# When a fused attention and feed-forward kernel makes the hidden layer of its next step: always a step ahead, or only while weights are converted

## The chip, the core and the metric

The kernel runs on one core of a Trainium2 chip. The core has a matmul engine (PE, with its weight loads shown as PEld), a vector engine (DVE), a scalar engine (ACT), GpSimd (POOL) and a queue for transfers (SP). The metric is the device time of one execution in microseconds; the time before is the median of three runs.

## What is computed

The reference is a chain of three parts: attention with a decay instead of a softmax, a feed-forward layer with the activation h * tanh(softplus(h)), and a layer of 8 experts with a greedy assignment of tokens that respects a capacity. All is float32. The change touches the second part, for which the first part delivers x.

```python
scores = scale * np.matmul(q, k.transpose(0, 1, 3, 2))
ret = scores * Dmat[None, :, :, :]          # decay, causal
x = np.matmul(ret, v)                       # -> 2304 tokens x 512
...
h = x @ w_in                                # 512 -> 2048
sp = np.where(h > 20.0, h, np.log1p(np.exp(np.minimum(h, 20.0))))
g = h * np.tanh(sp)
y = g @ w_out                               # 2048 -> 512
...
out[mask] = np.maximum(y[mask] @ w1[e], 0.0) @ w2[e]    # per expert e
```

## The kernel before

The kernel has a first part (attention and feed-forward, `first_part`) and a second one (ranking of tokens and experts). The first part takes tokens in 9 blocks n of 256 and the 2048 hidden features in 16 groups f of 128. One pair (n, f) is a step; `plan` (line 65) puts the 144 steps in order: the first 48 mix the blocks 0 to 2, while the weights of the layer still arrive and are converted, and from step 48 on the blocks follow one another. All matmuls work on float32 split into a high and a low part, three products for one.

A step is a chain through all engines:

- `ff_h` (line 310): PE makes h, 12 matmuls into half a PSUM bank `ph`. The halves of one bank hold an even step and the odd one behind it; there are two such banks, `ph0` and `ph1`. An h of an odd step waits for the tanh of the even one in its bank; an h of an even step waits until the products of the two steps that used the bank last are made (`ff_b2`, line 353).
- `ff_a1` (line 322): ACT takes tanh, a square and a scaling (lines 327 to 329) into `d`, DVE multiplies the halves of `d` (line 335). `ff_a2`: DVE takes the reciprocal (line 340).
- `ff_b1` (line 342): POOL makes two products (lines 347, 348). `ff_b2`: DVE makes the activation's value (line 353).
- `ff_b3` (line 355): ACT rounds it to `gh` (line 359), POOL makes the rest `gl` (line 360).
- `ff_y` (line 398): PE multiplies both with the second weight and accumulates y, 6 matmuls of 512 columns (line 412), or 12 of 256 in the last block (line 448). The matmuls with `gh` come first, those with `gl` fifth and sixth; in the last block `gl` is in every third.

The loop (line 532) is the order written out by hand; each engine executes its instructions in the order in which they are issued. In turn i it issues, in this sequence: the slots of step i (pieces of attention for later blocks, of router logits and the like, with matmuls on PE and evictions on ACT and DVE), `ff_a1` of step i, `ff_h` of step i + 1, `ff_b3` of step i - 2, `ff_a2` of step i, `ff_b2` of step i - 1, `ff_b1` of step i, and `ff_y` of step i - 3. So h is made one turn ahead of its elementwise work. The first h is made in turn 0.

While weights are converted, which takes much of ACT and DVE, `now` or `old` holds a conversion. By `CONV` (line 58) and the 32 pieces, the last conversion is taken up in turn 28; `now` or `old` is set in turns 0 to 30. In these turns POOL's share of the elementwise work lies on DVE.

Of the kernel before, what the change touches and what calls it, by code (L numbers as in the profile page):

```python
# [64 lines left out]
def plan():  # L65


    spread = lambda a, b, n: [a + (b - a) * k // (n - 1) for k in range(n)]
    own = {i: (0, f) for f, i in enumerate([0, 1, 2, 3] + spread(6, ENDS[0], NF - 4))}
    free = [i for i in range(3 * NF) if i not in own]  # L70
    lead = [i for i in free if i < BEGIN2]
    rest = [i for i in free if BEGIN2 <= i]
    near = [i for i in rest if i <= ENDS[1]]
    ones = lead + [near[k] for k in spread(1, len(near) - 1, NF - len(lead))]
    own.update({i: (1, f) for f, i in enumerate(ones)})
    own.update({i: (2, f) for f, i in enumerate(i for i in free if i not in ones)})
    steps = [own[i] for i in range(3 * NF)]
    steps += [(n, f) for n in range(3, NB) for f in range(NF)]
    return steps


def first_part(ctx, tc, att, att_ht, att_hn, dtab, qtab, ktab, stab, wi, wo, wgb, ydram, L, constants, cst, begin, grid):
# [16 lines left out]
    steps = plan()  # L99
# [42 lines left out]
    class convert:  # L142
# [18 lines left out]
        def x(self):  # L161
            w0 = self.w0
            nc.vector.scalar_tensor_tensor(w0, self.w1, 0x80000000, w0, op0=ALU.bitwise_and,  # L163
                                           op1=ALU.bitwise_or)
# [16 lines left out]
    def x_block(n):  # L181
        if n not in xT:
            if n == 2:
                xT[n] = [sp.tile([P, KT, TB], F32R, tag="x2", name=f"x{k}2", bufs=2) for k in "hl"]
            else:
                xT[n] = [work.tile([P, KT, TB], F32R, tag="x" + k, name="x" + k, bufs=2) for k in "hl"]
        return xT[n]
# [117 lines left out]
    q2 = {}  # L305
# [4 lines left out]
    def ff_h(n, f, i):  # L310
        xh, xl = x_block(n)
        if i % 2 == 0:
            hbank[0] = psum.tile([P, 2, TB], F32, tag=("ph0", "ph1")[i // 2 % 2], name="ph")
        ph = hbank[0][:, i % 2, :]
        k = 0
        for kt in range(KT):
            for w, x in ((winh, xh), (winl, xh), (winh, xl)):
                nc.tensor.matmul(ph, w[f][:, kt, :], x[:, kt, :], start=(k == 0), stop=(k == 11))  # L318
                k += 1
        q2[n, f] = ph  # L320

    def ff_a1(n, f, i, alone):

        ph = q2[n, f]
        d = work.tile([P, 2, P], F32, tag="d", name="d", bufs=2)
        df = d.rearrange("p a b -> p (a b)")
        nc.scalar.activation(df, ph, AF.Tanh, scale=0.5)  # L327
        nc.scalar.activation(df, df, AF.Square, bias=half_b, scale=-0.5)  # L328
        nc.scalar.activation(df, df, AF.Copy, bias=0.5, scale=0.5)  # L329
        u = work.tile([P, 2, P], F32, tag="u", name="u", bufs=3)  # L330
        r = u[:, 0, :]
        if alone:

            r = rs[:, i % 2 * P:][:, :P]
        nc.vector.tensor_mul(r, d[:, 0, :], d[:, 1, :])  # L335
        inv[n, f] = (d, u, r, alone)

    def ff_a2(n, f):
        r = inv[n, f][2]
        nc.vector.reciprocal(r, r)  # L340

    def ff_b1(n, f, eng):
        d, u, r, alone = inv.pop((n, f))
        if alone:
            eng.tensor_mul(u, d[:, ::-1, :], r[:, None, :].to_broadcast([P, 2, P]))
        else:
            eng.tensor_mul(u[:, 1, :], d[:, 0, :], r)  # L347
            eng.tensor_mul(u[:, 0, :], d[:, 1, :], r)  # L348
        gt[n, f] = u.rearrange("p a b -> p (a b)")

    def ff_b2(n, f):
        g = gt[n, f]
        nc.vector.scalar_tensor_tensor(g, g, -1.0, q2.pop((n, f)), op0=ALU.add, op1=ALU.mult)  # L353

    def ff_b3(n, f, eng):
        g = gt[n, f]
        gh = work.tile([P, TB], F32R, tag="gh", name="gh", bufs=3)
        gl = work.tile([P, TB], F32R, tag="gl", name="gl", bufs=3)
        nc.scalar.activation(gh, g, AF.Copy)  # L359
        eng.tensor_sub(gl, g, gh.bitcast(F32))  # L360
        gt[n, f] = (gh, gl)
# [152 lines left out]
    old, now, nxt = c2, c3, convert()  # L514
# [8 lines left out]
    for n in range(4, NB):  # L523
        ms = micro(n)
        for j, m in enumerate(ms):
            first = 5 if n == 4 else 1
            at = FOUR[j] if n == 4 else int(first + (14 - first) / len(ms) * j)
            slots.setdefault((n - 1) * NF + at, []).extend(m)

    for x in slots.get(-1, []):  # L530
        x()
    for i in range(len(steps) + YL):
        new = i < len(steps)
        if not i:
            ff_h(*steps[0], 0)
        if i == 20:
            constants()
        if i == 62:
            stage.__exit__(None, None, None)
            late = tc.tile_pool(name="late", bufs=1)  # L540
            WG = late.__enter__().tile([P, E, DM], F32, name="WG")
            nc.sync.dma_start(WG, wgb)
        if now:
            now.x()
            now.a()
        if old:
            old.l()
        if new:
            n, f = steps[i]
            for x in slots.get(i, []):  # L550
                x()
            if i and steps[i - 1] in inv:
                ff_b1(*steps[i - 1], nc.vector)
            ff_a1(n, f, i, bool(now or old))
            if i + 1 < len(steps):
                ff_h(*steps[i + 1], i + 1)
        if new:

            eng = nc.vector if now or old else nc.gpsimd
            if i > 1:  # L560
                ff_b3(*steps[i - 2], eng)
            ff_a2(n, f)
            if i:
                ff_b2(*steps[i - 1])
            if eng is not nc.vector:
                ff_b1(n, f, nc.vector if i == len(steps) - 1 else eng)
        if i == len(steps) - 1:
            ff_b2(n, f)
            ff_b3(*steps[i - 1], nc.gpsimd)
            ff_b3(n, f, nc.vector)  # L570
        if now:
            now.h()
        old, now = now, None
        if nxt and i in CONV:
            now, nxt = nxt, convert() if done[0] < len(parts) else None
            now.x1()
            now.c()
        for k in range(2 if i % 4 == 0 or TAIL <= i < POP2 else 1):
            if idle:
                idle.pop(0)()  # L580
        if late and i > TAIL + BEGIN and not idle:
            late = late.__exit__(None, None, None)
            soon.extend(begin())
        if i >= YL:
            ff_y(*steps[i - YL], i)
# [840 lines left out]
def build(tc, ap, out):  # L1426
    nc = tc.nc
    with ExitStack() as ctx:
        pp = ctx.enter_context(tc.tile_pool(name="pp", bufs=1))
        dp = ctx.enter_context(tc.tile_pool(name="dp", bufs=1, space=bass.MemoryType.DRAM))  # L1430
        cp = ctx.enter_context(tc.tile_pool(name="cp", bufs=1))
        ctx.enter_context(tc.manual_schedule())
        L = pp.tile([P, NT, E], F32, name="L")
        ydram = dp.tile([N, DM], F32, name="ydram")
        cst = {}
        start = []
        cs = ExitStack()

        def begin():
            start.append(Search(cs, tc, L, cst))  # L1440
            return start[0].early()

        with ExitStack() as c1:
            first_part(c1, tc, ap["att"], ap["att_ht"], ap["att_hn"], ap["dtab"], ap["qtab"],
                       ap["ktab"], ap["stab"], ap["wi"], ap["wo"], ap["wgb"], ydram, L, lambda: constants(cp, tc, ap, cst), cst, begin, lambda *a: Grid(cs, tc, L, cst).pieces(*a))
        keep = ctx.enter_context(tc.tile_pool(name="keep", bufs=1, reuse_waits="tile"))
        L0 = keep.tile([P, NT, E], F32, name="L0")
        nc.gpsimd.tensor_copy(L0, L)
        with ExitStack() as c2:
            flag = second_part(c2, tc, L, ydram, ap["wx"], cst, out, start[0], True, L0)  # L1450
            again = nc.values_load(flag[0:1, 0:1], min_val=0, max_val=1)
        cs.close()
        with tc.If(again != 0):
            with ExitStack() as c3:
                general_constants(c3, tc, ap, cst)
                second_part(c3, tc, L0, ydram, ap["wx"], cst, out, Start(c3, tc, L0, cst), False)
# [15 lines left out]
def constants(cp, tc, ap, cst):  # L1472
    nc = tc.nc
    load_constants(cp, tc, ap, cst, (("ident", [P, P], F32), ("J", [P, NJ + 1], F32), ("SCL", [P, 3], F32),
                                     ("pri", [P, E], F32), ("tri", [P, P], BF), ("io", [P, 96], BF),
                                     ("pcv", [P, NT, 2], BF), ("WGN", [P, KT, E], F32)))
    cst["ones"] = cp.tile([P, P], BF, name="c_ones")
    nc.vector.memset(cst["ones"], 1.0)
# [69 lines left out]
```

## Time and profile before

| | us |
|---|---|
| median of three runs (lowest, highest) | 843.76 (842.48, 844.92) |
| the profiled execution | 842.58 |
| its span | 840.7 |
| PE busy | 771.4 |
| DVE busy | 541.6 |
| POOL busy | 477.9 |
| ACT busy | 441.1 |

The busy times are sums over the whole span. The first part ends near 544 us; the steps without conversion, which the change touches, begin near 147 us. Matmuls overlap in a running stream and their ends are modelled, so the next start is the better mark for when one is through.

### The profile page before, as it was taken

What the parts mean: (1) busy time and instruction counts of PE and PEld (TensorE: products, weight loads), DVE (VectorE), ACT (ScalarE), POOL (GpSimd) and SP (SyncE); (2) the same over time, 40 slices, a digit from 0 to 9 for tenths busy, and PEclk for the clock granted to TensorE, in tenths of its full rate; (3) what the DMA queues carried; (4) which work ended last, traced back from release to release, by engine and by line L of the source; (5) the groups of instructions that cost most, each with busy time, mean ns of one, the idle gap of its engine ahead of it and who ended that gap; (6) DMA issues with size and microseconds to landing.
All of it is one profiled execution on the core that took longest, in us unless ns stands there. A gap on an engine that the chain in (4) does not pass through costs nothing.

```text
span 840.7 us, 16293 instructions
## 1 busy us (share of the span) xinstructions
PE 771.4 (92%) x6151; PEld 700.1 (83%) x6151; DVE 541.6 (64%) x1271; ACT 441.1 (52%) x963; POOL 477.9 (57%) x541
## 2 busy tenths in 40 slices
PE   6688999999999999999999999939999999999993
PEld 5677777888888887888888889929989999999993
DVE  4797999555645797887988976576566653442110
ACT  2678999544544554545555554423444543554520
POOL 2543333554445576666766655314777986977811
PEclk9799999999999999999999999958999999999997
DMA  8545442001312310310110000044565664655411
GB/s 315 190 136 202 152 159 101 27 1 51 101 51 101 107 44 2 101 51 27 51 51 26 1 27 2 8 164 143 168 183 180 190 195 155 187 163 170 125 30 32
DMA packets 27321, 87.63 MB, mean 104 GB/s; under 512 B 4449, under 2 KB 5601, under 8 KB 27105
## 3 DMA queue, kind: packets, MB, share of 16 engines
q1 hardware_dynamic: 24160, 77.06, 28.2%
q0 software_dynamic: 3072, 9.44, 3.5%
q8 instruction: 50, 0.82, 0.4%
q14 instruction: 39, 0.31, 0.1%
HBM read 77.05 MB, written 9.44 MB: 103 GB/s over the span
## 4 chain that ended last, share of the span: by engine, by line
PE 64%; DVE 18%; issue 7%; ACT 5%; POOL 2%; DMA 2%; SPq 0%; DVEq 0%; POOLq 0%; ACTq 0%
PE ph L318 18%; PE hp L1263 9%; PE op L1277 8%; PE b_F L412 6%; PE b_E L412 6%; DVE u L340 2%; DVE rs L340 2%; PE cnt L978 2%; DVE raw L163 2%; DVE y L168 1%; DVE u L353 1%; PE b_D L248 1%; DVE u L335 1%; PE b_A L219 1%; PE b_E L448 1%
## 5 line engine op out<-in xcount | busy, mean ns | idle before, releaser
L318 PE MATMUL ph<-xh,winh 128*128 128x256 f32 x576 | 170.5, 296 | 29.0 <-ACT d L327 21.4
L318 PE MATMUL ph<-xl,winh 128*128 128x256 f32 x576 | 161.6, 281 | 1.6 <-DVE xl L255 1.6
L318 PE MATMUL ph<-xh,winl 128*128 128x256 f32 x576 | 161.3, 280 | 0.0
L817 POOL TENSOR_TENSOR wxl<-wraw,wxh 128x1024 fp32r<-128x1024 f32 x60 | 142.3, 2397 | 29.9 <-ACT wxh L815 29.5
L318 PEld LDWEIGHTS ph<-xh,winh 128*128 128x128 f32 x576 | 109.1, 189 | 49.6 <-ACT d L327 28.0
L360 POOL TENSOR_TENSOR gl<-u,gh 128x256 fp32r<-128x256 f32 x114 | 88.6, 778 | 88.0 <-ACT gh L359 87.4
L318 PEld LDWEIGHTS ph<-xh,winl 128*128 128x128 f32 x576 | 109.7, 191 | 2.0
L318 PEld LDWEIGHTS ph<-xl,winh 128*128 128x128 f32 x576 | 109.4, 190 | 2.1 <-DVE xl L255 2.1
L340 DVE RECIPROCAL u<-u 128x128 f32<-128x128 f32 x113 | 107.7, 953 | 3.9
L327 ACT ACTIVATE d<-ph 128x256 f32<-128x256 f32 x144 | 54.5, 379 | 98.1 <-PE ph L318 84.2
L347 POOL TENSOR_TENSOR u<-d,u 128x128 f32<-128x128 f32 x112 | 52.4, 468 | 58.8 <-DVE u L340 58.7
L335 DVE TENSOR_TENSOR u<-d 128x128 f32<-128x128 f32 x113 | 48.3, 427 | 46.4 <-ACT d L329 42.8
L815 ACT ACTIVATE wxh<-wraw 128x1024 fp32r<-128x1024 f32 x64 | 67.3, 1052 | 17.1 <-DMA wraw<-in_wx_dram 17.0
L328 ACT ACTIVATE d<-d,half_b 128x256 f32<-128x256 f32 x144 | 73.5, 511 | 4.7
L348 POOL TENSOR_TENSOR u<-d,u 128x128 f32<-128x128 f32 x112 | 68.2, 609 | 8.8
L359 ACT ACTIVATE gh<-u 128x256 fp32r<-128x256 f32 x144 | 58.5, 406 | 11.3 <-DVE u L353 9.3
L329 ACT ACTIVATE d<-d 128x256 f32<-128x256 f32 x144 | 60.2, 418 | 4.5
L369 DVE SCALAR_TENSOR_TENSOR scr<-y,WG 128x512 bf16<-128x512 f32 x64 | 55.2, 862 | 0.4
L1254 DVE SCALAR_TENSOR_TENSOR htl<-hp,hth 128x288 fp32r<-128x288 f32 x64 | 28.4, 454 | 40.3 <-ACT hth L1266 39.8
L1266 ACT ACTIVATE hth<-hp 128x288 fp32r<-128x288 f32 x64 | 26.1, 408 | 52.3 <-PE hp L1263 51.8
L353 DVE SCALAR_TENSOR_TENSOR u<-u,ph 128x256 f32<-128x256 f32 x144 | 52.5, 365 | 0.3
L1263 PE MATMUL hp<-xth,wxh 128*128 128x288 f32 x256 | 50.2, 309 | 0.9 <-DVE htl L1254 0.9
(271 smaller groups left out, 1885.6 us busy)
## 6 DMA issues: line engine op xcount, KB each, us to landing
wraw<-in_wx_dram SPq DMA_DIRECT2D x64, 512.0 KB, 4.4
att<-in_att_dram SPq DMA_DIRECT2D x32, 512.0 KB, 5.0
raw<-in_wi_dram SPq DMA_DIRECT2D x16, 512.0 KB, 3.3
raw<-in_wo_dram SPq DMA_DIRECT2D x16, 512.0 KB, 3.3
ydram<-y SPq DMA_DIRECT2D x9, 512.0 KB, 2.8
WG<-in_wgb_dram SPq DMA_DIRECT2D x1, 2048.0 KB, 7.6
att<-in_att_ht_dram SPq DMA_DIRECT2D x4, 256.0 KB, 3.8
att<-in_att_hn_dram SPq DMA_DIRECT2D x4, 256.0 KB, 4.1
```

The lines of the kernel that those rows point to most:

```text
L318: nc.tensor.matmul(ph, w[f][:, kt, :], x[:, kt, :], start=(k == 0), stop=(k == 11))
L328: nc.scalar.activation(df, df, AF.Square, bias=half_b, scale=-0.5)
L329: nc.scalar.activation(df, df, AF.Copy, bias=0.5, scale=0.5)
L340: nc.vector.reciprocal(r, r)
L348: eng.tensor_mul(u[:, 0, :], d[:, 1, :], r)
L353: nc.vector.scalar_tensor_tensor(g, g, -1.0, q2.pop((n, f)), op0=ALU.add, op1=ALU.mult)
L360: eng.tensor_sub(gl, g, gh.bitcast(F32))
L412: nc.tensor.matmul(py[n][t], g[:, t * P:(t + 1) * P], w[f], start=(f == 0 and w is woh and g is gh), stop=(f == NF - 1 and g is gl))
L815: nc.scalar.activation(hi, raw, AF.Copy)
L817: rest = lambda eng: eng.tensor_sub(lo, raw, hi.bitcast(F32))
L1263: nc.tensor.matmul(hp, W[kt][w][:, s], x[:, kt, :], start=(k == 0), stop=(k == 11))
L1277: nc.tensor.matmul(op, W[4 + ft // 2][w][:, s], h[:, ft, :], start=(k == 0), stop=(k == 23))
```

## The change

A function `not_yet` tells whether the h of a step has not been made. At the head of turn i the h of step i is made if it is missing. Behind `ff_a1`, the h of step i + 1 is made only if the turn has a conversion (`now` or `old`). So turns 0 to 30 make the h of steps 1 to 31 as before; the h of the steps 32 to 143 is made at the head of its own turn, ahead of the slots. The instructions are the same; on DVE, ACT, POOL and SP their order is the same as well. On PE each of these 112 h changes places with the y that stood behind it.

```diff
+    not_yet = lambda i: steps[i] not in q2
     for x in slots.get(-1, []):
         x()
     for i in range(len(steps) + YL):
         new = i < len(steps)
-        if not i:
-            ff_h(*steps[0], 0)
+        if not i or new and not_yet(i):
+            ff_h(*steps[i], i)
...
             ff_a1(n, f, i, bool(now or old))
-            if i + 1 < len(steps):
+            if now or old:
                 ff_h(*steps[i + 1], i + 1)
```

PE at the seam, where the first moved h stands. `ph` is h of a step, `b_A` to `b_F` are banks that accumulate y (or hold attention pieces); the last rows of one y and the first of the next are shown with the h around them, and the lines with + and - are the after and the before.

```order
 L412 MATMUL b_A<-woh_121,gl 128x512
 L412 MATMUL b_B<-woh_121,gl 128x512
+L412 MATMUL b_E<-woh_113,gh 128x512
+L412 MATMUL b_E<-wol_129,gh 128x512
+L412 MATMUL b_F<-woh_113,gh 128x512
+L412 MATMUL b_F<-wol_129,gh 128x512
+L412 MATMUL b_E<-woh_113,gl 128x512
+L412 MATMUL b_F<-woh_113,gl 128x512
 L318 MATMUL ph<-xh,winh_91 128x256
 L318 MATMUL ph<-xh,winl_107 128x256
```

The y that stood behind this h (of step 32) now stands ahead of it, right behind the y of the step before.

PE around step 46, with the semaphores waited for: end of a y (`woh_122`), the attention output of a chunk (L243, L248), h of step 47 (`winh_91`) and a y (`woh_120`). Before:

```order
L412 MATMUL b_D<-woh_122,gl 128x512
L243 MATMUL b_A<-att,sd 128x128 [waits PE_49]
L243 MATMUL b_A<-att,sd 128x128 x3
L248 MATMUL b_A<-pm,att 64x128 [waits DMAHW4_49]
L248 MATMUL b_A<-pm,att 64x128 x7
L318 MATMUL ph<-xh_602,winh_91 128x256 [waits Activation_49]
...
L412 MATMUL b_E<-woh_120,gh 128x512
```

After, from the same attention output on:

```order
L243 MATMUL b_A<-att,sd 128x128 [waits PE_49]
L243 MATMUL b_A<-att,sd 128x128 x3
L248 MATMUL b_A<-pm,att 64x128 [waits DMAHW4_49]
L248 MATMUL b_A<-pm,att 64x128 x7
L412 MATMUL b_E<-woh_120,gh 128x512 [waits Activation_49]
...
L412 MATMUL b_E<-woh_120,gl 128x512 [waits Pool_49]
L412 MATMUL b_F<-woh_120,gl 128x512
L318 MATMUL ph<-xh_602,winh_91 128x256 [waits Activation_49]
```

The y of six matmuls has come between the attention output and the h that waits for ACT.

PE at the end of the phase, with the last h (step 143, `winh_91`). Before:

```order
L448 MATMUL b_F<-gl,woh_118 128x256
L318 MATMUL ph<-xh,winh_91 128x256 [waits Activation_49]
...
L318 MATMUL ph<-xl,winh_91 128x256
L448 MATMUL b_E<-gh,woh_119 128x256
...
L448 MATMUL b_E<-gh,woh_120 128x256 [waits Activation_49]
```

After:

```order
L448 MATMUL b_E<-gl,woh_119 128x256 [waits Pool_49]
...
L448 MATMUL b_F<-gl,woh_119 128x256
L318 MATMUL ph<-xh,winh_91 128x256 [waits Activation_49]
...
L318 MATMUL ph<-xl,winh_91 128x256
L448 MATMUL b_E<-gh,woh_120 128x256 [waits Activation_49]
```

Five y stood behind the last h (`woh_119` to `woh_123`); now four do.

## Rows read from the trace of the kernel before

**Rows 1.** The page's busy line: us, share of the span, instructions of each engine.

```profile
PE 771.4 (92%) x6151; PEld 700.1 (83%) x6151; DVE 541.6 (64%) x1271; ACT 441.1 (52%) x963; POOL 477.9 (57%) x541
```

**Rows 2.** Busy time by stretch: us, each engine's us, granted clock, DMA share, GB/s.

```profile
147.00:285.00 138.00, 132.06 (x979) 116.02 (x978) 75.23 (x139) 66.33 (x165) 68.26 (x116) 1.00 0.17 61
285.00:489.00 204.00, 200.32 (x1521) 174.79 (x1520) 175.10 (x352) 107.88 (x260) 135.75 (x196) 1.00 0.12 41
489.00:544.00 55.00, 54.04 (x439) 52.22 (x438) 33.10 (x78) 27.28 (x67) 27.18 (x49) 1.00 0.03 11
```

**Rows 3.** The page's chain that ended last, by engine and line.

```profile
PE ph L318 18%; PE hp L1263 9%; PE op L1277 8%; PE b_F L412 6%; PE b_E L412 6%; DVE u L340 2%; DVE rs L340 2%; PE cnt L978 2%; DVE raw L163 2%; DVE y L168 1%; DVE u L353 1%; PE b_D L248 1%; DVE u L335 1%; PE b_A L219 1%; PE b_E L448 1%
```

**Rows 4.** PE's waits from 147 to 545 us: us in total, times, longest.

```profile
PE ph L318 <- ACT d L327: 7.3, 8, 1.0
PE ph L318 <- DVE u L353: 2.8, 7, 0.5
PE b_A L382 <- ACT y L421: 0.5, 1, 0.5
```

**Rows 5.** Timeline at step 46: start, us, engine, instruction, idle before it.

```profile
202.67 0.39 PE L248 MATMUL b_A<-pm,att 128*64 128x128 f32 x4
203.11 0.60 ACT L254 ACTIVATE xh<-b_A 128x512 fp32r<-128x512 f32 x1 [4.59 <-PE b_A L248]
203.60 0.38 ACT L327 ACTIVATE d<-ph 128x256 f32<-128x256 f32 x1
...
204.03 0.39 PE L318 MATMUL ph<-xh,winh 128*128 128x256 f32 x1 [0.97 <-ACT d L327]
```

**Rows 6.** Timeline of a plain step in the last block, step 138.

```profile
519.93 0.28 PE L448 MATMUL b_E<-gh,woh 128*128 128x256 f32 x1
...
520.20 0.38 ACT L327 ACTIVATE d<-ph 128x256 f32<-128x256 f32 x1 [1.14 <-PE ph L318]
...
521.35 0.28 PE L318 MATMUL ph<-xh,winh 128*128 128x256 f32 x1
...
521.48 0.40 ACT L359 ACTIVATE gh<-u 128x256 fp32r<-128x256 f32 x1
...
521.96 0.73 POOL L360 TENSOR_TENSOR gl<-u,gh 128x256 fp32r<-128x256 f32 x1 [0.74 <-ACT gh L359]
...
522.76 0.28 PE L448 MATMUL b_E<-gh,woh 128*128 128x256 f32 x1
```

**Rows 7.** Timeline beside attention products: gl, h and y around step 69's y.

```profile
298.19 1.29 POOL L228 TENSOR_TENSOR att<-att,qt 128x512 f32<-128x512 f32 x1
...
300.30 0.28 PE L318 MATMUL ph<-xh,winh 128*128 128x256 f32 x1
300.50 0.73 POOL L360 TENSOR_TENSOR gl<-u,gh 128x256 fp32r<-128x256 f32 x1
...
301.69 0.39 PE L412 MATMUL b_E<-woh,gh 128*128 128x512 f32 x1
```

**Rows 8.** Timeline of the same at step 63.

```profile
279.19 0.74 POOL L360 TENSOR_TENSOR gl<-u,gh 128x256 fp32r<-128x256 f32 x1
...
280.93 0.39 PE L412 MATMUL b_E<-woh,gh 128*128 128x512 f32 x1
```

**Rows 9.** Timeline of the same at step 36.

```profile
173.26 0.73 POOL L360 TENSOR_TENSOR gl<-u,gh 128x256 fp32r<-128x256 f32 x1
...
175.20 0.39 PE L412 MATMUL b_E<-woh,gh 128*128 128x512 f32 x1
```

**Rows 10.** Line 360 on POOL, 150 to 545 us: ns least, median, most.

```profile
L360 POOL TENSOR_TENSOR gl<-u,gh x113: 721/741/1197, 151.4 to 538.0; 128x256 fp32r<-128x256 f32 x113
```

**Rows 11.** Timeline at the end of the phase.

```profile
534.33 0.38 ACT L327 ACTIVATE d<-ph 128x256 f32<-128x256 f32 x1 [1.14 <-PE ph L318]
...
537.46 0.42 ACT L359 ACTIVATE gh<-u 128x256 fp32r<-128x256 f32 x1 [1.45 <-DVE u L353]
...
537.95 0.74 POOL L360 TENSOR_TENSOR gl<-u,gh 128x256 fp32r<-128x256 f32 x1 [1.13 <-ACT gh L359]
...
538.75 0.38 PE L448 MATMUL b_E<-gl,woh 128*128 128x256 f32 x1
```

## The prediction

> **What bounds the kernel now.** Read the busy line first [rows 1]: the matmul engine (PE) is busy for 771.4 of 840.7 us, no other engine for more than 542. Then the stretches [rows 2]: the change touches steps 32 to 143 of the first part, which lie between about 147 and 544 us. There PE is busy 132.06 of 138, 200.32 of 204 and 54.04 of 55 us at a granted clock of 1.00, so the most that can be had from this stretch is its idle time plus a little, about 11 us, and no clock is to be won. The vector engine (DVE) has 175.10 of 204 in the middle, 86%, so it has room, though not much. The chain that ended last runs through the h-matmuls (L318) and the y-matmuls (L412) [rows 3]; what delays PE here delays the end.
>
> Third, who keeps PE waiting there [rows 4]: h for ScalarE's (ACT's) tanh, 8 times, 7.3 us; h for DVE's L353, 7 times, 2.8 us; once a transpose for ACT's copy of y, 0.5 us. No y appears in the list at all. The sum of gaps is 10.6 us. PE's ends are modelled: in an undisturbed stream the next matmul starts about 0.16 us before the end shown of the last (in [rows 6] y starts every 2.83 us with one 1.42 us y and one 1.41 us h between, without a gap). A wait takes away this overlap too: 16 x 0.15 = 2.4 us more. The waits cost about 13.0 us.
>
> Look at one [rows 5]. PE ends the attention products of step 46 (L248) at 203.06. ACT copies them to xh at 203.11, and only then comes to the tanh of step 46 (203.60 to 203.98), though its h had long been made. h of step 47 shares a PSUM bank with h of step 46 and waits for that tanh: it starts at 204.03, after 0.97 idle. Between the two stands no other PE work: that is what the order before makes, attention pieces directly followed by the next h.
>
> **What the change does to it.** It adds and removes no instruction. In steps 32 to 143 (112 of 144) the h of a step changes places with the y that stood behind it. Attention pieces keep their place: the same PE work lies ahead of them before and after. So each h has one y more ahead of it (1.42 us later) and each y one h less (1.41 us earlier), both as seen from the other work. ACT, DVE, POOL and SP keep their order.
>
> *h-waits.* What h waits for can move later by no more than h itself, since a tanh moves only if it waited for its own h. Hence no h-wait grows. The longest of the 16 costs 0.97 + 0.24 = 1.21 us, less than the y now in front of it. In the case of [rows 5] tanh does not move at all (it stands behind the xh copy), y runs from about 203.0 to 204.4, and the bank is free 0.4 us before that. The seven DVE waits cost at most 0.63 each; their DVE work may move by up to 0.7 and still fits into 1.41. The transpose gets an h between itself and y. All 16 go: **-13.0 us**; I bound it by -10.6 (gaps alone) and -13.4 (with partial waits hidden in the overlap).
>
> *y-waits in plain steps.* Each y loses 1.41 us ahead of it, and its inputs come up to 1.41 later. The steps near 520 show what is left [rows 6]: the tanh of step 138 starts at 520.20, gh of step 136 (L359) is done at 521.88, gl (L360, POOL) at 522.69. Counting from 519.93, where the h of step 138 gives way to the next stream, that is 1.95 and 2.76. After the change y and h stand between that h and y of step 136, 2.83 us. gh has 0.88 to spare. gl is needed by the third of twelve matmuls of a y in the last block (2/12 of 1.41, 0.24 later) and by the fifth of six in the blocks before (4/6, 0.94 later): 0.31 and 1.01 to spare. **0**, as long as nothing on ACT, DVE or POOL is slower than these rows.
>
> *y-waits next to attention.* In eight steps POOL multiplies both q and k (L228, L233) ahead of gl; in seven of these gl is close, in three kinds. The closest [rows 7]: gl ends at 301.23; its y starts at 301.69 and needs gl at 302.63, 1.40 to spare. Now y starts where h stood, at 300.30, and needs gl at 301.24: nothing to spare. Two are like this. Three have 1.94 before (gl ends at 279.93, y starts at 280.93) and two have 2.15 (173.99 and 175.20) [rows 8, 9], so 0.5 and 0.7 after, if POOL's work does not move. It should not: the products wait for the scores, which keep their place. If all of POOL's work moved by the full 1.41, each spare would fall by 2.82 and the seven would wait 2 x 1.42 + 3 x 0.88 + 2 x 0.67 = 6.8 us. The bounds are 0 and 6.8. I take **+0.7**, near the lower end, for the two without spare and some jitter.
>
> *The end of the phase.* Before, five y follow the last h without any h between; now four do, while the chain behind the last h is as long [rows 11]. The tanh of step 143 starts at 534.33 and gh of step 142 ends at 537.88, gl at 538.69; already now y of 142 waits for gl, its third matmul starting at 538.75. The last h moves by 1.42, so this gl comes at 540.11, its third matmul starts near 540.15 instead of 538.75, and the rest follows: **+1.4**, less 0.1 because the wait there takes the place of the present one: +1.3. It is bounded by 0 and 1.42.
>
> *The seam to step 32.* y of step 28 moves ahead of h of step 32; by the same count gh has 0.9 to spare there: 0.
>
> Sum: -13.0 + 0.7 + 1.3 = **-11.0 us**. The profiled execution took 842.58 us (its span 840.7); it lies 1.2 below the median of the three timed, 843.76. So 831.6 for a run like the profiled one, and 832.7 for the median, -1.3%. What follows 544 us starts from the last y, and I let it move as a whole.
>
> **The rivals.**
>
> *A: POOL is late at y.* The wait on tanh gives way to a wait on gl. gl takes 721 ns at least, 741 in the middle and 1197 at most [rows 10], so something sometimes holds POOL up by 0.46. Priced by the full 6.8: -13.0 + 6.8 + 1.3 = -4.9, 838.9. For it speaks that two y have no spare; against it that POOL's products hang on scores that stay. [...]
>
> *B: slower.* The loop h(j+2), tanh, gh(j), y(j), h(j+4) now spans two steps and has 0.88 spare [rows 6]. If ACT's chain in its own turn came 1.2 us later than the rows say, through DVE at 86% in the middle stretch [rows 2], each loop of two steps would lose 0.3: 56 loops give 16.8, so -13.0 + 1.3 + 16.8 = +5.1, 848.9. It turns the sign from 0.21 lost per loop on, 1.09 later than in the rows. Against it: before, PE waited for the inputs of a y nowhere in the list of 397 us [rows 4], and the elementwise work moves as one piece.
>
> *C: no change.* The phase ends earlier but what follows waits for something that does not move (a transfer, the ranking on DVE), or new small waits eat all: 843.8. Against it: the chain passes from y straight into the products behind it [rows 3], and transfers take 3% of the time just ahead of it [rows 2].
>
> **How the numbers follow.** Forecast 66%, with its own range 829.5 to 835 (13.4 won with no new wait less the spread of the runs; 10.6 won with 1.3 lost and some waiting); A 16%, B 9%, C 9%. The range for 8 in 10 takes in the forecast and A: 829.5 to 839. Faster by over 0.3% (2.5 us, about what a measurement of this kernel can tell): forecast and A, 0.82; within: C, 0.09; slower: B, 0.09.
>
> **What would show it.** In the profile after, L318 waits for L327 and L353 under 1.5 us in total between 147 and the phase's end; L412 and L448 show waits for ACT or POOL, under 3 us; the ranking behind the phase (L978) begins about 11 us earlier; at the end, the y-matmuls after the last h have over 1 us of gaps. A list with y-waits on L360 of 5 us means A; y-waits on L359 in every second step mean B; the phase shorter and the total unchanged mean C. The sum fails if attention pieces or the evictions of y turn out to stand on what the swapped y or h delays.

## The result and the profile after

| | before | changed |
|---|---|---|
| median, us (lowest, highest) | 843.12 (840.72, 844.92), 4 runs | 831.83 (831.35, 832.36), 4 runs |
| ratio to before, 95% interval | | 0.9868 (0.9841 to 0.9895) |
| profiled execution, us | 842.58 | 831.90 |
| its span, us | 840.7 | 830.1 |

In a later comparison on one chip the changed kernel took 832.46 us against 841.89, a ratio of 0.9896 (0.9876 to 0.9915). So the change makes the kernel faster by 9.4 to 11.3 us.

The busy time by stretch of the changed kernel (us, each engine's us with instructions, granted clock, DMA share, GB/s) answers to [rows 2]:

```profile
147.00:285.00 138.00, 138.00 (x1030) 123.93 (x1029) 79.02 (x151) 70.39 (x175) 72.86 (x123) 1.00 0.18 62
285.00:489.00 204.00, 204.00 (x1547) 182.05 (x1546) 173.82 (x354) 106.33 (x261) 135.55 (x200) 1.00 0.12 42
489.00:533.00 44.00, 42.12 (x351) 40.97 (x350) 25.74 (x62) 20.84 (x51) 21.37 (x38) 1.00 0.01 4
```

The matmul engine (PE) is shown busy all the time from 147 to 489 us. The granted clock is 1.00 there as it was. The last 44 us have 1.9 us of idle time, where [rows 2] had 1.0 in 55.

Who keeps PE waiting between 147 and 545 us, in the changed kernel (us in total, times, longest); this answers to [rows 4]. The rows of `cnt`, `rp` and `dg` belong to the ranking behind the phase; lines behind the edit are numbered one higher than before:

```profile
PE cnt L979 <- DVE ind L694: 2.3, 2, 1.2
PE rp L916 <- DVE rs L1022: 2.0, 1, 2.0
PE b_D L645 <- DVE g_mm L641: 1.0, 1, 1.0
PE dg L989 <- DVE full L983: 0.5, 2, 0.3
PE b_E L448 <- POOL gl L360: 0.5, 2, 0.3
PE b_E L448 <- ACT gh L359: 0.4, 1, 0.4
```

No h (L318) is in the list any more. New are the waits of y (L448), at the end of the phase only, and that of a small transpose, L645.

The place of [rows 5], step 46, in the timeline of the changed kernel:

```profile
199.07 1.09 PE L248 MATMUL b_A<-pm,att 128*64 128x128 f32 x16
200.10 0.50 PE L412 MATMUL b_E<-woh,gh 128*128 128x512 f32 x1
200.22 0.60 ACT L254 ACTIVATE xh<-b_A 128x512 fp32r<-128x512 f32 x1 [2.98 <-PE b_A L248]
...
200.71 0.38 ACT L327 ACTIVATE d<-ph 128x256 f32<-128x256 f32 x1
...
201.60 0.28 PE L318 MATMUL ph<-xh,winh 128*128 128x256 f32 x1
```

ACT does exactly what it did: the copy of xh, and only then the tanh, which ends at 201.09. But PE makes a y meanwhile, and h starts at 201.60 with no idle time, half a microsecond after its bank was free.

### The profile page after: what moved, and what is told of

Same layout as the page of the kernel before. It is cut to its first block, busy times and chain, and to the rows that moved or that the text cites. A ratio compares the mean times of both kernels' runs of the same rounds, so it can differ in the third digit from the quotient of the medians.

```text
span 830.1 us, 16295 instructions
## 1 busy us (share of the span) xinstructions
PE 771.4 (93%) x6151; PEld 706.2 (85%) x6151; DVE 538.0 (65%) x1271; ACT 437.5 (53%) x963; POOL 476.6 (57%) x541
## 4 chain that ended last, share of the span: by engine, by line
PE 73%; DVE 12%; issue 7%; ACT 3%; POOL 2%; DMA 2%; SPq 0%; DVEq 0%; POOLq 0%; ACTq 0%
PE ph L318 21%; PE hp L1264 9%; PE b_E L412 8%; PE op L1278 8%; PE b_F L412 8%; DVE rs L340 2%; PE cnt L979 2%; DVE raw L163 2%; PE b_A L219 2%; DVE y L168 1%; PE b_D L248 1%; DVE hot L875 1%; PE b_E L448 1%; PE b_F L448 1%; PE b_D L243 1%
## 5 line engine op out<-in xcount | busy, mean ns | idle before, releaser
L318 PE MATMUL ph<-xh,winh 128*128 128x256 f32 x576 | 165.4, 287 | 19.1 <-ACT d L327 14.2
L318 PE MATMUL ph<-xl,winh 128*128 128x256 f32 x576 | 162.4, 282 | 1.6 <-DVE xl L255 1.6
L318 PE MATMUL ph<-xh,winl 128*128 128x256 f32 x576 | 162.2, 282 | 0.0
L360 POOL TENSOR_TENSOR gl<-u,gh 128x256 fp32r<-128x256 f32 x114 | 85.9, 753 | 91.9 <-ACT gh L359 91.2
L318 PEld LDWEIGHTS ph<-xh,winh 128*128 128x128 f32 x576 | 109.5, 190 | 32.6 <-ACT d L327 18.6
L318 PEld LDWEIGHTS ph<-xh,winl 128*128 128x128 f32 x576 | 109.9, 191 | 4.2
L318 PEld LDWEIGHTS ph<-xl,winh 128*128 128x128 f32 x576 | 110.4, 192 | 2.1 <-DVE xl L255 2.1
L335 DVE TENSOR_TENSOR u<-d 128x128 f32<-128x128 f32 x113 | 44.1, 391 | 64.5 <-ACT d L329 59.3
L347 POOL TENSOR_TENSOR u<-d,u 128x128 f32<-128x128 f32 x112 | 52.3, 467 | 50.9 <-DVE u L340 50.8
L348 POOL TENSOR_TENSOR u<-d,u 128x128 f32<-128x128 f32 x112 | 68.2, 609 | 8.8
L369 DVE SCALAR_TENSOR_TENSOR scr<-y,WG 128x512 bf16<-128x512 f32 x64 | 55.3, 863 | 0.4
L353 DVE SCALAR_TENSOR_TENSOR u<-u,ph 128x256 f32<-128x256 f32 x144 | 52.5, 365 | 0.3
```

## The experiments

Two theories stood against each other. The first: PE waited because an attention piece (or a router piece) was directly followed by an h whose bank ACT, busy with that piece, had not read yet; the change wins by putting a y between, and pays at y and at the end. The second: the win is in h and its own work standing closer together. For all stretches given below, a start in the trace of one profiled execution is compared with the same start in another.

### y one turn later

```diff
-YL = 3
+YL = 4
-LOG2 = (3, 4, 6)
+LOG2 = (4, 5, 7)
```

The second line keeps three router pieces of block 7 behind the y that they read.

> The changed kernel with y issued one turn later still (y of step i-4 in turn i). PE then does h, slots, y with the same y between an attention piece and the next h as in the changed kernel, but each y has the room back that it had before the change, and five y follow the last h again. Theory 1 (the gain is the y that now covers the wait of h behind an attention piece; the price is the shorter way from the last h to the end): the h-waits stay gone, and the phase ends about 1.3 us earlier than in the changed kernel, some 830.5 us. Theory 2 (the gain comes from h and its y standing closer together): half of it or more is lost, 836 or more.

It took 838.61 us (ratio to before 0.9955, 0.9938 to 0.9971). By its time this looks like the second theory. The trace says otherwise. Its waits of PE from 147 to 545 us, the two largest:

```profile
PE b_F L412 <- DVE y L422: 3.0, 4, 0.8
PE cnt L979 <- DVE ind L694: 1.2, 1, 1.2
```

The h-waits stay gone, as the first theory wanted. What is lost is lost in two other places. One is the change of a block, here with the two engines:

```profile
281.67 0.28 PE L318 MATMUL ph<-xh,winh 128*128 128x256 f32 x1
...
284.46 0.50 PE L412 MATMUL b_F<-woh,gh 128*128 128x512 f32 x1 [0.73 <-DVE y L422]
```

```profile
282.58 0.95 DVE L340 RECIPROCAL u<-u 128x128 f32<-128x128 f32 x1
283.45 0.36 DVE L353 SCALAR_TENSOR_TENSOR u<-u,ph 128x256 f32<-128x256 f32 x1
283.73 0.68 DVE L422 COPY y<-b_F 128x512 f32<-128x512 f32 x1
```

The copy of a finished y out of its bank stands on DVE behind the products of its turn, and the first y of the next block needs the bank. In the changed kernel the same pair has an attention piece between, since its turn holds a slot (in its timeline, `283.00 0.69 PE L273`, then `283.62 0.51 PE L412`); one turn later there is none. By starts this costs 3.7 us. The other place is the turns with conversion: h of step 32 starts at 150.62 against 149.06, although one y of 1.41 less lies ahead of it, so 3.0 us are lost there. They are lost at one spot. From h of step 5 to h of step 7 it takes 12.28 us (47.70 to 59.98), in the changed kernel 9.27 (49.22 to 58.49). The trace of this run there, and its granted clock from 54.07 to 57.20:

```profile
50.05 1.40 POOL L177 TENSOR_TENSOR winl<-y,winh 128x512 fp32r<-128x512 f32 x1 [1.29 <-ACT winh L174]
50.23 1.37 DVE L335 TENSOR_TENSOR rs<-d 128x128 f32<-128x128 f32 x1
51.40 1.09 POOL L233 TENSOR_TENSOR att<-att,kt 64x512 f32<-64x512 f32 x1
51.52 1.25 DVE L360 TENSOR_TENSOR gl<-u,gh 128x256 fp32r<-128x256 f32 x1
...
54.07 0.55 PE L318 MATMUL ph<-xh,winh 128*128 128x256 f32 x1 [1.43 <-DVE u L353]
```

```profile
54.07:57.20 3.13, 3.13 (x14) 3.03 (x15) 3.03 (x6) 2.07 (x4) 1.15 (x1) 0.50 0.27 81
```

Two DVE products start just behind the start of a POOL instruction and end just behind its end: 1.37 and 1.25 us. In the changed kernel the same two take 0.28 and 0.41 (at 50.92 and 51.13), and there it is POOL's L177 that takes longer (1.93 at 50.76). h of step 6 waits 1.43 us for the L353 behind the two. In the 3.13 us from its start the granted clock is 0.50, where the changed kernel has 1.00 in the same window, and its 12 matmuls take 2.69 us instead of 1.49. Why the order of y shifts DVE and POOL against each other there, and what lowers the clock, is not shown. There is one trace of this order, but scatter is unlikely: from h of step 5 to h of step 31 this run takes 98.79 us, while four executions whose first 131 turns are those of the changed kernel (two of it and two of its variants below) take 95.71 to 95.78. The second theory has no support left: nothing of the loss is at an h of the steps that the change moved.

### tanh ahead of the slots, h where it was

```diff
             n, f = steps[i]
+            first = not (now or old)
+            if first:
+                ff_a1(n, f, i, False)
             for x in slots.get(i, []):
                 x()
...
-            ff_a1(n, f, i, bool(now or old))
+            if not first:
+                ff_a1(n, f, i, bool(now or old))
```

This is the kernel before, with h a step ahead. It takes away what h waits for, instead of covering the wait.

> The kernel before, with h a step ahead as it was, but in turns without conversion the tanh part of a step (ACT lines 327 to 329 and the DVE product, line 335) issued ahead of the slots instead of behind them. Theory 1: the eight waits of h for tanh go (7.3 us of gaps, 8.5 with the overlap), those for DVE's line 353 stay or shift by a little, so about 834.5 us. Theory 2: no gain without moving h, 843.

It took 829.14 us (0.9838, 0.9822 to 0.9854). So the late reads on ACT and DVE were the cause, and the waits can be removed without moving an h or a y. The tanh and the DVE product behind it moved together; what each of them is worth was not tried alone. My number was too cautious: the waits for DVE's line 353 went as well. The same kernel run again beside the changed kernel:

> The run e2_tanh_first once more beside the changed kernel: 829.1, that is 2 to 3 us below the changed kernel. The sum by its trace: the same waits of h gone (12 of 13 us), and neither the end of the phase (1.3) nor the small transpose of the grid (1.1) paid.

It took 828.46 us, where the changed kernel took 832.46: 4.0 us less. What is left of PE's waits in the steps from 147 us on:

```profile
PE ph L318 <- ACT d L327: 0.7, 1, 0.7
...
PE b_A L382 <- ACT y L421: 0.5, 1, 0.5
```

Both are waits behind a copy of y (L421). In its timeline at step 46 h follows the attention piece at once and waits for nothing, because ACT has had the tanh behind it before the piece ends:

```profile
197.72 0.42 ACT L329 ACTIVATE d<-d 128x256 f32<-128x256 f32 x1
...
198.86 1.09 PE L248 MATMUL b_A<-pm,att 128*64 128x128 f32 x16
199.88 0.38 PE L318 MATMUL ph<-xh,winh 128*128 128x256 f32 x1
200.00 0.60 ACT L254 ACTIVATE xh<-b_A 128x512 fp32r<-128x512 f32 x1 [1.87 <-PE b_A L248]
```

### The end of the phase, given back

```diff
-            if now or old:
+            if now or old or TAIL + 6 <= i < len(steps) - 1:
                 ff_h(*steps[i + 1], i + 1)
```

> The changed kernel, but from turn 134 on h is made a step ahead again, so that five y follow the last h as before the change; in turn 134 the logit products (L392) stand between the two h made there. Theory 1: the gaps of y behind the last h (1.39 us in the trace of the changed kernel against 0.32 before) go back to 0.3 and the end comes 1.0 to 1.4 us earlier, 830.6. If the end is not set by this chain, no change, 831.8.

It took 830.49 us (0.9857, 0.9841 to 0.9874), 1.3 us below the changed kernel. In its trace the y behind the last h wait 0.2 us by starts, and from h of step 128 to the ranking it takes 57.20 us against 58.70. With `TAIL + 3` in place of `TAIL + 6`:

> The changed kernel, but with h a step ahead again from turn 131 on instead of from turn 134 as in the run e3_tail. Beside the chain at the end this puts an h ahead of the small transpose of the grid (L645), which waits 0.98 us for DVE in the changed kernel and did not before. If this wait is a price of the change, it goes and the time is 1.0 us below that run, about 829.5; h made in turn 131 may wait for its bank, up to 0.5 us. If the wait is of another origin, 830.5.

It took 829.07 us (0.9849, 0.9826 to 0.9872). From h of step 128 to the ranking 56.73 us are left. The wait of L645 is gone; two h wait 0.2 and 0.4 by starts for their bank, which takes back half of what it gave. So the price of L645 is shown by the trace; the medians, taken on different chips, differ by 1.4, and their intervals overlap.

### h in its own turn everywhere

```diff
-        if not i or new and not_yet(i):
+        if new:
             ff_h(*steps[i], i)
...
-            if now or old:
-                ff_h(*steps[i + 1], i + 1)
```

> The changed kernel with h made in its own turn in all steps, those with conversions too. There DVE and ACT are nearly full and PE already waits, so one theory says h comes too late for ACT: every conversion turn waits for its own h, up to 1.4 us in 30 turns, some 10 to 40 us slower than the changed kernel. The other says these turns are bound by DVE whatever PE does, and the time is that of the changed kernel within 2 us.

It took 835.46 us (0.9916, 0.9897 to 0.9936), 3.6 above the changed kernel: less than the first theory and more than the second. The loss is all ahead of step 32, whose h starts at 152.41 against 149.06; from there to the ranking both take 385.5 to 385.7 us. In its trace from 10 to 152 us:

```profile
PE ph L318 <- ACT d L327: 9.2, 11, 3.0
PE b_C L412 <- ACT woh L174: 4.5, 1, 4.5
```

The h wait less for tanh there (the changed kernel has 14.2 us, 12 times), but y now waits once for its weights, which are just being converted. Between h of step 7 and h of step 8 6.1 us are lost, part of which comes back in the next steps; over the 152.41 us ahead of h of step 32 the granted clock is 0.93 on average, where the changed kernel has 0.95 over its 149.06.

### How much room y had, and has

```diff
         eng.tensor_sub(gl, g, gh.bitcast(F32))
+        if eng is nc.gpsimd:
+            eng.tensor_sub(gl, g, gh.bitcast(F32))
```

The same product twice on POOL, 0.74 us more in each step, in three orders.

> The kernel before with one more POOL instruction of about 0.74 us in each of the 113 steps whose gl is made on POOL: the same product gl is made twice. It measures how much room y has. If, as the rows say, gl has 1.4 us or more to spare in every step, nothing waits for it and the time stays within 1 us; POOL's busy time rises by some 84 us.

> The changed kernel with the same additional POOL instruction. By the rows a plain step has 1.0 us to spare in the blocks up to the seventh (no wait) and 0.31 in the last block (0.4 per step in some 10 steps), and seven steps beside attention have 0 to 0.7 (0 to 0.74 each): 5 to 9 us slower than the changed kernel, some 839. If y had as much room as before the change, it stays at 832.

> The run e2_tanh_first (h a step ahead, the tanh part of a step ahead of its slots) with the additional POOL product of e5. There the burden cost the kernel before some 4 us and the changed kernel some 18. If the difference is the room of y that the change spent, this order, which moves no y, pays like the kernel before: 829 + 4, some 833 to 836. If the burden costs any kernel that no longer waits for tanh about the same, 847.

| order | without | with | the burden costs |
|---|---|---|---|
| before | 841.80 | 846.27 | 4.5 |
| changed | 831.83 | 849.97 | 18.1 |
| tanh ahead of the slots | 828.46 | 832.28 | 3.8 |

Beside the second measurement of the changed kernel (832.46) its burden costs 17.5. Both of my first numbers were too low. I had counted the room of each gl singly, but the product also delays POOL's own work of the same step behind it (L347, L348), and with it the buffers that the next tanh needs: in the kernel before, ACT's tanh waits for L348 8.4 us without the burden (13 times) and 51.5 with it (39 times). The comparison holds all the same: one and the same burden costs the changed order four times what it costs the others. In the changed order with the burden, PE waits for gl (147 to 560 us; with the added lines L414 is L412, L450 is L448, and L362 is the second gl):

```profile
PE b_E L414 <- POOL gl L362: 6.3, 11, 1.5
PE b_E L450 <- POOL gl L362: 2.7, 6, 1.1
```

With tanh ahead of the slots and the burden, it hardly does:

```profile
PE b_E L450 <- POOL gl L362: 0.6, 2, 0.4
```

The room can be read from the traces without the burden too, as the time from the end of a gl to the start of the first matmul that reads it. Over the 99 steps 29 to 127 its least and middle values are 1.37 and 3.41 us before, 0.10 and 1.69 in the changed kernel, and 1.96 and 3.67 with tanh ahead of the slots. Under 0.74 us lie 26 steps of the changed kernel and none of the other two.

The change has bought its 11 us with the room of y. As long as nothing on POOL is slower, that costs nothing; a slower ACT was not tried.

### One more step

```diff
-LOG2 = (3, 4, 6)
+LOG2 = (4, 5, 7)
```

on top of the order with tanh ahead.

> The run e2_tanh_first with the three logit pieces of block 7 one turn later (LOG2 4, 5, 7), so that the transpose of y (L382) no longer stands straight behind the y whose eviction it waits for (0.6 us). If that wait simply goes, 0.6 us below e2_tanh_first, 828.5; the uncertainty of the runs may hide it, the profile shows it.

It took 828.35 us (0.9843, 0.9823 to 0.9862) beside 828.46: no difference that these runs can tell. The wait of L382 is gone from its list. Both of these orders are faster than the kernel before and the changed one.

## Why the prediction was right, point by point

It said 832.7 us, from a sum of -11.0; the medians moved by 11.3 and in the repetition by 9.4, the profiled executions by 10.7.

**The h-waits, -13.0.** Right. All sixteen are gone. By the starts of matmuls in the trace of before, against undisturbed neighbours, the sixteen had cost 12.9 us. That none grew elsewhere, because what h waits for can move by no more than h, holds: the list above has no L318. Why they stood there is settled by the order with tanh ahead of the slots, which removes fourteen of the sixteen by other means; it keeps one h-wait and that of the transpose (L382).

**y in plain steps, 0.** Right. No y-wait from 147 to 489 us is worth a line in the list. The room was smaller than the rows said: three steps without attention products on POOL (76, 108 and 124) have 0.33 us from the end of gl to the matmul that reads it, where the sum had 1.01. The steps of [rows 6] did not stand for all.

**y beside attention, +0.7.** Too high by about 0.6: only 0.14 us can be found, for a copy of y, not for gl. The tightest place was forecast to have no spare, and so it is. In the timeline of the changed kernel, y of step 69 and its gl, which answers to [rows 7]:

```profile
291.14 1.30 POOL L228 TENSOR_TENSOR att<-att,qt 128x512 f32<-128x512 f32 x1
...
293.36 0.40 PE L412 MATMUL b_E<-woh,gh 128*128 128x512 f32 x1
293.47 0.73 POOL L360 TENSOR_TENSOR gl<-u,gh 128x256 fp32r<-128x256 f32 x1
...
294.25 0.19 PEld L412 LDWEIGHTS b_E<-woh,gl 128*128 128x128 f32 x1 [0.23 <-POOL gl L360]
```

gl ends at 294.20 and its weight load starts at 294.25; the load waits, the matmul behind it shows no gap. POOL's attention products kept their place, which is what the choice near the lower bound rested on. Rival A, with all of POOL's work moved, is out. gl took 724 ns at least, 737 in the middle and 912 at most, no slower than in [rows 10]. What ran beside POOL's slowest gl, the trace of before shows. The longest one there:

```profile
427.67 0.83 DVE L369 SCALAR_TENSOR_TENSOR scr<-y,WG 128x512 bf16<-128x512 f32 x1
427.91 1.20 POOL L360 TENSOR_TENSOR gl<-u,gh 128x256 fp32r<-128x256 f32 x1
...
428.43 0.82 DVE L335 TENSOR_TENSOR u<-d 128x128 f32<-128x128 f32 x1
```

All seven gl of over 0.95 us start 0.24 to 0.44 us behind the start of such a logit product on DVE (L369). In the rows shown the DVE product behind it (L335), which takes 0.28 us in a plain step, takes 0.82 and ends just behind gl (429.25 and 429.11). What links the two engines is not shown. In the changed kernel every gl that meets an L369 starts ahead of it or 0.55 us and more behind its start and takes 0.73 to 0.87, so beside them gl took no more time than before and mostly less.

**The end, +1.3.** Right, and by the mechanism named. The end of the phase in the changed kernel, which answers to [rows 11]:

```profile
524.53 0.38 ACT L327 ACTIVATE d<-ph 128x256 f32<-128x256 f32 x1 [1.15 <-PE ph L318]
...
526.26 0.39 PE L448 MATMUL b_E<-gh,woh 128*128 128x256 f32 x1 [0.42 <-ACT gh L359]
...
527.07 0.38 PE L448 MATMUL b_E<-gl,woh 128*128 128x256 f32 x1 [0.30 <-POOL gl L360]
...
528.88 0.39 PE L448 MATMUL b_E<-gl,woh 128*128 128x256 f32 x1 [0.17 <-POOL gl L360]
```

From the start of the last h to the logits behind the phase it takes 8.81 us, before 8.94, with one y of 1.41 less in it: 1.28 lost. Putting h ahead again for the last turns gave 1.3 back.

**What the sum left out.** Two things of about 1 us each, both a loss. The first is a piece of work on PE that is neither h, y nor a slot: the pieces from `idle`, issued at the end of a turn. They stood behind the h made ahead and now stand without it. L645, a small transpose, needs a reduction by DVE (L639 to L641), which stands behind the L353 of the same turn:

```profile
490.47 0.15 DVE L641 TENSOR_SCALAR g_mm<-g_mm 128x1 f32<-128x1 f32 x1
...
490.77 0.27 PE L645 MATMUL b_D<-c_ident,g_mm 128*2 128x128 f32 x1 [0.98 <-DVE g_mm L641]
```

Before, this matmul (L644 there) followed an h and waited for nothing. "Attention pieces keep their place" was true of the slots and not checked for these. Cost: 1.1 us by starts. The second is the spacing of undisturbed matmuls: those of y start 0.231 us apart where it was 0.229, over some 460 of them 0.8 us, and those of h 0.1164 where it was 0.1155, over some 1240 of them 1.1 us. The order with tanh ahead of the slots keeps 0.229 and 0.1155. I have no explanation for it that a run shows. Against it stand 1.2 us won on the second matmul behind a wait, which starts late and goes with the wait (see the last section).

Together: -12.9, +0.1, +1.3, +1.1, +0.8, +1.1 and -1.2 make -9.7; from h of step 31 to the ranking the traces differ by 9.6 us (399.4 to 389.9). The remaining 1.0 of the spans lies ahead of the stretch (0.3) and behind it (0.7), where the programs are alike. So the total came out as close as it did partly by luck: +0.7 for y, which was not needed, stood in for part of the 1.8 that were missed, and 1.0 came from outside the stretch.

**The rivals.** B, the loop that runs out of room at gh, did not happen. A slower kernel was near all the same, by way of gl: with 0.74 us more on POOL per step the changed order takes 849.97 us, more than the kernel before without it, 841.80. C, a phase that ends earlier with nothing won, is out: the ranking starts at 534.79 instead of 544.71.

## What to carry to other kernels

When a matmul waits for an engine that is merely late to an instruction it could have done long ago, look first at the order on that engine: issuing the read of a shared bank ahead of the evictions won some 13 us here and cost no room, where moving the matmuls won 9 to 11 and spent it. When two streams change places, list everything else that stood behind either of them, the small pieces at the end of a turn too, and count the last turns by themselves. Room that a change spends shows in no list of waits. The time from a producer's end to its reader's start shows it, and a known burden, put into both orders, measures what it is worth.

## What the runs showed of the hardware

A wait cost more here than its gap in the list: the sixteen of before have gaps of 10.6 us and cost 12.9 by starts. In a running stream the next matmul starts some 0.16 us before the modelled end of the last (the median in both traces from 147 to 489 us), and this overlap goes with the wait; besides, a second matmul starts 0.11 us late: behind a wait or a row of small ones 0.22 us behind the first instead of 0.115 for h of 256 columns (before), and behind a row of small ones 0.34 instead of 0.23 for y of 512 (changed kernel). Two instructions were longer beside one of another engine, with no wait in the trace: gl 1.20 us beside L369 instead of 0.74, L335 1.37 us beside L177 instead of 0.28. And the four executions named above differ ahead of the steps more than in them: h of step 5 starts anywhere from 48.87 to 50.23 us, while the 26 steps from there to h of step 31 take 95.71 to 95.78.
